# Seven products of halves in the first MLP stage of the last two units

## The chip, the cores and the metric

The kernel runs on one core of one Trainium2 chip. The metric is device time in microseconds (us), the median of several runs. TensorE does the matmuls (its weight loads have a row of their own, PEld), VectorE (DVE), ScalarE (ACT) and GpSimd (POOL) do the rest; SP issues most DMAs. L-numbers are lines of the kernel before.

## The reference

For 8 batches with 8 heads, 576 positions and 64 values per head: k and v are averaged over groups of 8 positions (72 remain), `x = softmax(q k^T / 8) v` per head, and the heads side by side give x with 576 rows of 512. Then a token MLP and a channel MLP:

```python
h  = np.maximum(xt @ w_tok1, 0.0) @ w_tok2        # over the 576 tokens, 256 hidden
u  = x + h.transpose(0, 2, 1)
h2 = np.maximum(u @ w_ch1, 0.0) @ w_ch2           # 512 -> 1536 -> 512
return u + h2
```

## The kernel before

The order of all work is written out by hand. `HEAD` lists the steps of the start. After it come nine units, 0 to 8, one for the channel MLP of 512 rows each: units 0 to 7 take 512 rows of one batch, unit 8 takes the remaining 64 rows of all eight batches (the tails). A unit is a Python generator, `unit_fast`, that stops (`yield`) after every four matmuls of 256 columns or two of 512. `PLAN[n]` maps the number of such a stop, here called a step, to other work that is put in there: `"6.av3"` is step av3 of batch 6. An engine executes its instructions in the order in which they were written down, so the position of a step is its position in the queue of every engine that it uses, DMA issues included.

**First stage of a unit.** `l1_tile` computes one of 12 tiles of `relu(u @ w_ch1)`, transposed: four matmuls of 128x512 (L517) add up in a PSUM bank, and ScalarE writes the relu to `GT` (L521). `uT` is u transposed, four chunks of 128 with 512 columns. 24 steps.

**Second stage.** It is already a product of 2x2 blocks with seven multiplications in place of eight (Winograd's form): `product` makes twelve matmuls of 256 columns (L583) for each of x, y, z, a second x, w, a second z and a third x, 21 steps. In unit 8 w is left for the end and added up in x's bank. `plus` adds the bank of a product to the residual or to an earlier sum (L626: `s` tiles and output tiles `o`). Sums of blocks of GT are made by `g_sums` on VectorE, named in the plan as `=1` to `=4` (L545, L557); those of `w_ch2` are made once, in unit 0.

**The attention steps of a later batch** fill a unit: K and V pool keys and values on GpSimd (L174 to L180), Q transposes q, s computes scores and their exponentials, av the weighted values (L379, scaled on VectorE in L384), at and u the token MLP (L393, L415, L416). From batch 3 on, uT is made over memory: M0, M2 and M4 write u out, M and MT read it back in quads of 32 rows, and T0 to T5 transpose it in blocks on VectorE (L458; T4 and T5 are the tails). l steps load the inputs of a later batch.

**gate** (`g` in the plan) is a small VectorE memset (L712) and a GpSimd copy that waits for it (L713). The next gate's memset waits for that copy, so neither engine runs far ahead of the other.

**PSUM** has eight banks: four single ones (p1a to p1d), handed out in turn by `take` and `give`, and two tiles of two banks (`ps_two`). A bank is written again when its reader is done.

Of the kernel before, what the change touches and what calls it, by code (L numbers as in the profile page):

```python
# [8 lines left out]
FP32 = mybir.dt.float32  # L9
BF16 = mybir.dt.bfloat16  # L10
U32 = mybir.dt.uint32
AF = mybir.ActivationFunctionType
# [19 lines left out]
]  # L32
# [3 lines left out]
def kernel(  # L36
# [14 lines left out]
    nc = tc.nc  # L51
    B, H, S, D = q.shape
    P = 128
    POOL = 8
    BOUNCED = range(3, B)
    SP = S // POOL
# [48 lines left out]
    qT0 = area[:, 3200:3200 + 2 * HP * EV].rearrange("m (a l n) -> m a l n", a=HP, l=2)  # L105


    values = [singles.tile([SP, H, D + 1], BF16, name=f"vp{i}") for i in range(2)]
    exps = [singles.tile([SP, H * S + BP], BF16, name=f"ex{i}") for i in range(2)]
    rests = [singles.tile([P, DM], BF16, name=f"xt{i}") for i in range(2)]  # L110
# [76 lines left out]
    def batch_steps(b):  # L187
# [136 lines left out]

        def avh(g, c):
            def go():
                cs = (c, c + 1) if c < 4 else (4,)
                ps = ps_two.tile([P, 2, 512], FP32, name="p2")
                den = outp.tile([P, 2, 4], FP32, name="den", bufs=4)
                for i, cc in enumerate(cs):  # L330
                    for h in range(4):
                        n0 = (4 * g + h) * S + cc * P
                        nc.tensor.matmul(out=ps[:, i, h * (D + 1):(h + 1) * (D + 1)], lhsT=st["ex"][:, n0:n0 + P],
                                         rhs=st["vp"][:, 4 * g + h, :], start=True, stop=True)
                view = ps[:, :, 0:4 * (D + 1)].rearrange("p a (h e) -> p a h e", e=D + 1)
                if c < 4:
                    dst = late("x")[:, c:c + 2, g * 256:(g + 1) * 256].rearrange("p c (h d) -> p c h d", d=D)
                    nc.vector.reciprocal(out=den, in_=view[:, :, :, D])
                    nc.vector.tensor_tensor(out=dst, in0=view[:, :, :, 0:D],
                                            in1=den[:, :, :, None].broadcast_to([P, 2, 4, D]), op=ALU.mult)  # L340
                else:
                    nc.vector.reciprocal(out=den[0:BP, 0], in_=view[0:BP, 0, :, D])
                    nc.vector.tensor_tensor(out=st["xt"][0:BP, g * 256:(g + 1) * 256].rearrange("p (h d) -> p h d", d=D),
                                            in0=view[0:BP, 0, :, 0:D], in1=den[0:BP, 0, :, None].broadcast_to([BP, 4, D]),
                                            op=ALU.mult)
            return go
# [22 lines left out]

        def av(c):  # L370
            def go():
                n0 = c * P if c < 4 else (8 * BP if par == 0 else 7 * BP)
                rows = slice(0, P) if c < 4 else lower
                n = rows.stop - rows.start
# [9 lines left out]
                nc.vector.tensor_tensor(out=dst.rearrange("p (a h d) -> p a h d", a=2, d=D),  # L384
                                        in0=view[:, :, :, 0:D],
                                        in1=den[rows, :, :, None].broadcast_to([n, 2, 4, D]), op=ALU.mult)
            return go
# [105 lines left out]
        for i in range(3):  # L493
            name[f"s{i}"] = scores(i)
        for c in range(5):
            name[f"av{c}"], name[f"u{c}"], name[f"t{c}"] = av(c), u(c), uT(c)
            for g in range(2):
                name[f"a{g}{c}"], name[f"m{g}{c}"] = avh(g, c), ath(g, c)
        for c in range(6):
# [14 lines left out]
    def l1_tile(n, m, uT):  # L514
        ps = take([P, 512], FP32)
        for kk in range(4):
            nc.tensor.matmul(out=ps, lhsT=w_ch1[:, kk, m * P:(m + 1) * P], rhs=uT[kk],  # L517
                             start=(kk == 0), stop=(kk == 3))
            if kk == 1:
                yield  # L520
        nc.scalar.activation(out=GT[:, m, :], in_=ps, func=AF.Relu)  # L521
        give(ps)
        yield
# [19 lines left out]

    def sub(out, a, b):
        nc.vector.tensor_tensor(out=out, in0=a, in1=b, op=ALU.subtract)  # L545

# [4 lines left out]

    def g_sums(s):
        S4 = sums_tile("S", "area")
        if s[0] == "3":
            sub(S4[:, 2], GT[:, f, lo], GT[:, f, hi])
        elif s[0] == "1":
            nc.vector.tensor_tensor(out=S4[:, 0], in0=GT[:, f, hi], in1=GT[:, sec, hi], op=ALU.add)  # L557
        elif s[0] == "2":
            sub(S4[:, 1], S4[:, 0], GT[:, f, lo])
        else:  # L560
            sub(S4[:, 3], GT[:, sec, lo], S4[:, 1])

    def weight_sum(k):
# [7 lines left out]
        else:  # L571
            sub(T[:, 3], w_ch2[:, sec, lo], T[:, 1])

    def unit_fast(n, u):
        last = n == B
        uT = [u["uT"][:, kk, :] for kk in range(4)]
        for m in range(NM):
            yield from l1_tile(n, m, uT)

# [62 lines left out]
        s1 = keep("s1")  # L642
        yield from product(x, lambda m: GT[:, m, lo], lambda m: w_ch2[:, m, lo], True,
                           plus(part(s1), part(x), residual(0, 0)), last)
        yield from product(y, lambda m: GT[:, NH + m, lo], lambda m: w_ch2[:, NH + m, lo], True,
                           plus(cols_of(oa, 0), part(y), part(s1)), end=y)
# [7 lines left out]
        if not last:  # L654
            w = bank()
            s4 = keep("s4")
            yield from product(w, lambda m: GT[:, NH + m, hi], lambda m: TW[:, 3, m], True,
                               plus(part(s4), part(w), residual(1, 0)), end=w)
# [3 lines left out]
        if last:  # L662
            yield from product(x, lambda m: SG[:, 2, m], lambda m: TW[:, 2, m], False,
                               plus(cols_of(ob, 1), part(x), part(s5), store_part(hi, [nc.scalar])), True)
            yield from product(x, lambda m: GT[:, NH + m, hi], lambda m: TW[:, 3, m], False,
                               plus(cols_of(ob, 0), part(x), residual(1, 0), store_part(lo, [nc.scalar, nc.sync])), True)
# [48 lines left out]
    def unit(n, at):  # L715
# [3 lines left out]
        for i, _ in enumerate(unit_fast(n, st)):  # L719
            for s in at.get(i, "").split():  # L720
                if s[0] == "=":
                    g_sums(s[1:])
                elif s == "g":
                    gate()
                elif s[0] == "w":
                    weight_sum(int(s[1:]))
                else:
                    b, s = s.split(".")
                    if s[0] == "l":
                        load(s[1], int(b))  # L730
                    else:
                        batches[int(b)][1][s]()

    with tc.manual_schedule(engines={PE, POOLE, DVE, ACT, SYNC}):
# [16 lines left out]
        for n in range(B + 1):  # L751
            unit(n, PLAN[n])

# [29 lines left out]
```

## Time and profile before

| | |
|---|---|
| runs | 265.91, 266.49, 267.24 us; median 266.49 |
| span of the profiled execution | 264.4 us; the runs' times lie 1.5 to 2.8 us above it |
| busy TensorE, VectorE, ScalarE, GpSimd | 256.2, 178.4, 119.6, 153.1 us |
| granted TensorE clock, mean | 0.999 |
| unit 6 begins, unit 7 begins, unit 8 begins | 196.6, 221.2, 240.7 us |
| last matmul ends, last VectorE add ends | 260.9, 261.35 us |

The time of the profiled execution is its span; what a run's own time has beyond it lies outside the instructions. A line of a group gives line, engine, operation, tiles, shape and count, then busy us and mean ns of one, then the idle time of the engine ahead of them and what ended it. A line of the timeline begins with start and length in us; instructions that follow each other are merged. The end of a matmul is modelled and reaches past the start of the next one, so starts are the better measure.

### The profile page before, as it was taken

What the parts mean: (1) busy time and instruction counts of PE and PEld (TensorE: products, weight loads), DVE (VectorE), ACT (ScalarE), POOL (GpSimd) and SP (SyncE); (2) the same over time, 40 slices, a digit from 0 to 9 for tenths busy, and PEclk for the clock granted to TensorE, in tenths of its full rate; (3) what the DMA queues carried; (4) which work ended last, traced back from release to release, by engine and by line L of the source; (5) the groups of instructions that cost most, each with busy time, mean ns of one, the idle gap of its engine ahead of it and who ended that gap; (6) DMA issues with size and microseconds to landing.
All of it is one profiled execution on the core that took longest, in us unless ns stands there. A gap on an engine that the chain in (4) does not pass through costs nothing.

```text
span 264.4 us, 5328 instructions
## 1 busy us (share of the span) xinstructions
PE 256.2 (97%) x2121; PEld 160.3 (61%) x2121; DVE 178.4 (67%) x370; ACT 119.6 (45%) x195; POOL 153.1 (58%) x177
## 2 busy tenths in 40 slices
PE   8799999989999999999999999999999999999994
PEld 3685466744677545774487447744874486486483
DVE  3557569996787655895599678844795576184183
ACT  2355763149536456425641575165435412612700
POOL 8577326899999999988959982898200010100000
PEclk9999999999999999999999999999999999999999
DMA  6999999993088928699447940830513053404104
GB/s 141 193 195 206 205 207 208 205 216 80 4 129 141 166 82 171 149 202 266 91 132 107 232 144 17 158 94 4 159 38 122 30 170 80 121 0 102 59 0 159
DMA packets 31704, 34.29 MB, mean 130 GB/s; under 512 B 3136, under 2 KB 23744, under 8 KB 31680
## 3 DMA queue, kind: packets, MB, share of 16 engines
q0 software_dynamic: 17632, 17.64, 42.3%
q1 hardware_dynamic: 13632, 15.93, 20.2%
q10 hardware_dynamic: 416, 0.39, 0.5%
q8 instruction: 16, 0.26, 0.4%
q14 instruction: 8, 0.07, 0.1%
HBM read 38.99 MB, written 12.58 MB: 195 GB/s over the span
## 4 chain that ended last, share of the span: by engine, by line
PE 73%; DVE 12%; POOL 8%; issue 3%; DMA 2%; ACT 1%; POOLq 0%; ACTq 0%
PE p1c L517 10%; PE p1b L517 8%; PE p1a L517 7%; PE p1d L517 7%; PE p1d L583 6%; PE p1c L583 5%; PE p1b L583 4%; PE p1a L583 4%; POOL t L174 3%; PE p L297 3%; DVE x L384 3%; DVE area L545 3%; PE p L379 2%; DMA kr<-in_k_dram 2%; POOL t L175 2%
## 5 line engine op out<-in xcount | busy, mean ns | idle before, releaser
L517 PEld LDWEIGHTS <-w_ch 128*128 128x128 bf16 x432 | 39.5, 98 | 44.4 <-issue 2.7
L713 POOL COPY flag<-flag 1x1 f32<-1x1 f32 x47 | 15.3, 326 | 86.0 <-DVE flag L712 86.0
L583 PEld LDWEIGHTS <-area 128*128 128x128 bf16 x432 | 41.4, 98 | 7.8 <-issue 1.2
L306 ACT ACTIVATE ex<-p 72x768 bf16<-72x768 f32 x42 | 31.6, 803 | 17.1 <-PE p L297 17.1
L583 PEld LDWEIGHTS <-GT 128*128 128x128 bf16 x324 | 30.7, 98 | 7.9 <-issue 1.6
L175 POOL TENSOR_TENSOR t<-t 72x512 f32<-72x512 f32 x23 | 31.2, 1358 | 1.8
L517 PE MATMUL p1c<-uT,w_ch 128*128 128x512 bf16 x116 | 31.4, 379 | 0.0
L521 ACT ACTIVATE GT<-p1b 128x512 bf16<-128x512 f32 x27 | 16.1, 597 | 27.5 <-PE p1b L517 20.9
L521 ACT ACTIVATE GT<-p1c 128x512 bf16<-128x512 f32 x32 | 19.1, 598 | 15.5 <-PE p1c L517 11.7
L517 PE MATMUL p1b<-uT,w_ch 128*128 128x512 bf16 x96 | 26.0, 379 | 0.0
L174 POOL TENSOR_TENSOR t<-kr 72x1024 f32<-72x1024 bf16 x12 | 25.5, 2121 | 0.4
L174 POOL TENSOR_TENSOR t<-vr 72x1024 f32<-72x1024 bf16 x11 | 23.4, 2125 | 1.0 <-DMA vr<-in_v_dram 0.5
L517 PE MATMUL p1a<-uT,w_ch 128*128 128x512 bf16 x88 | 23.9, 379 | 0.0
L517 PE MATMUL p1d<-uT,w_ch 128*128 128x512 bf16 x84 | 22.2, 379 | 0.0
L521 ACT ACTIVATE GT<-p1a 128x512 bf16<-128x512 f32 x25 | 14.9, 597 | 15.4 <-PE p1a L517 14.8
L521 ACT ACTIVATE GT<-p1d 128x512 bf16<-128x512 f32 x24 | 14.4, 599 | 12.8 <-PE p1d L517 7.3
L384 DVE TENSOR_TENSOR x<-p,den 128x512 bf16<-128x512 f32 x28 | 19.3, 691 | 1.0
L545 DVE TENSOR_TENSOR area<-GT 128x1536 bf16<-128x1536 bf16 x9 | 11.3, 1257 | 11.9 <-ACT GT L521 6.7
L557 DVE TENSOR_TENSOR area<-GT 128x1536 bf16<-128x1536 bf16 x9 | 9.5, 1054 | 11.3 <-ACT GT L521 11.3
L379 PEld LDWEIGHTS <-ex 72*128 72x128 bf16 x280 | 12.9, 98 | 6.5 <-DVE x L384 1.4
L379 PE MATMUL p<-vp,ex 72*128 72x65 bf16 x280 | 14.4, 194 | 0.3 <-POOL vp L180 0.2
L118 POOL DMA_DIRECT2D kr<-in_k_dram x17 | 10.9, 646 | 5.6 <-PE p1b L222 1.9
(185 smaller groups left out, 464.2 us busy)
## 6 DMA issues: line engine op xcount, KB each, us to landing
out_dram<-o SPq DMA_DIRECT2D x32, 256.0 KB, 4.2
qb<-in_q_dram POOLq DMA_DIRECT2D x7, 576.0 KB, 9.4
kr<-in_k_dram POOLq DMA_DIRECT2D x7, 512.0 KB, 8.4
vr<-in_v_dram POOLq DMA_DIRECT2D x7, 512.0 KB, 14.0
w_ch<-in_moe_w_ch_dram POOLq DMA_DIRECT2D x5, 512.0 KB, 14.8
mem<-u SPq DMA_DIRECT2D x10, 256.0 KB, 2.2
v<-mem SPq DMA_DIRECT2D x20, 128.0 KB, 2.9
area<-in_q_dram SPq DMA_DIRECT2D x2, 288.0 KB, 3.0
```

The lines of the kernel that those rows point to most:

```text
L118: nc.gpsimd.dma_start(out=t[j0:j1, h0:h1].rearrange("j h i d -> j h (i d)"), in_=src[b, h0:h1].rearrange("h (j i) d -> j h (i d)", i=POOL) ...
L174: eng.tensor_tensor(out=t4[:, 0:n], in0=t[:, hs, 0:4], in1=t[:, hs, 4:8], op=ALU.add)
L175: eng.tensor_tensor(out=t4[:, 0:n, 0:2], in0=t4[:, 0:n, 0:2], in1=t4[:, 0:n, 2:4], op=ALU.add)
L306: nc.scalar.activation(out=dst, in_=src, func=AF.Exp, scale=scale)
L379: nc.tensor.matmul(out=ps[:, h // 4, (h % 4) * (D + 1):(h % 4 + 1) * (D + 1)], lhsT=st["ex"][:, h * S + n0:h * S + n0 + P], rhs=st["vp"][: ...
L384: nc.vector.tensor_tensor(out=dst.rearrange("p (a h d) -> p a h d", a=2, d=D), in0=view[:, :, :, 0:D], in1=den[rows, :, :, None].broadcast ...
L517: nc.tensor.matmul(out=ps, lhsT=w_ch1[:, kk, m * P:(m + 1) * P], rhs=uT[kk], start=(kk == 0), stop=(kk == 3))
L521: nc.scalar.activation(out=GT[:, m, :], in_=ps, func=AF.Relu)
L545: nc.vector.tensor_tensor(out=out, in0=a, in1=b, op=ALU.subtract)
L557: nc.vector.tensor_tensor(out=S4[:, 0], in0=GT[:, f, hi], in1=GT[:, sec, hi], op=ALU.add)
L583: nc.tensor.matmul(out=ps[i] if split else ps[:, i], lhsT=chunk(u, i, a(m)), rhs=w(m), start=start and m == 0 and (i == 0 or split), stop= ...
L713: nc.gpsimd.tensor_copy(out=flag[:, 1:2], in_=flag[:, 0:1])
```

## The change

- In the units named in `FAST` (7 and 8, those whose uT sums y0 or Y0 stand in the plan) the first stage is also computed by seven products in place of eight. `w_ch1` is split in two halves of hidden units and two halves of inputs, uT in two halves of inputs and two of rows. `l1_fast` makes them in three groups A, B, C of four hidden tiles each. A step is four matmuls of 256 columns (`"A6"`: product 6 of group A), 21 steps in the order `ORDER`, and three empty steps behind them so that the plan's numbers stay. Per group products 1, 6, 7 and 4 add up in one bank and 2, 5 and 3 in another. ScalarE copies three interim sums to SBUF as 32-bit floats (`keep`); VectorE adds bank and copy into GT for three of the four blocks (`add`), with the relu as an in-place maximum behind it, once for groups A and B together and once for C; the fourth block is a relu on ScalarE as before.
- The copies lie in the two `ex` tiles, now 128 partitions high.
- The sums of `w_ch1` (`ch1_sum`) are four GpSimd instructions of 1536 in unit 6 (Z0 to Z3). Those of uT (`u_sum`) are y0 and y1 on VectorE, Y2 and Y3 on GpSimd for unit 7, and y0 to y3 on VectorE for unit 8.
- `GT` is laid out as two halves of rows, each contiguous, in every unit.
- The plans of units 6 to 8 are new: av0, av4, at1 earlier, at0 one step later, `=3` later, M4 behind M, MT later, T4 and T5 in unit 7's second stage. The option to scale av on ScalarE is not used by the plan.

The core of the diff:

```diff
-    {7: "7.av0", 10: "7.av4", 14: "7.at0 =3", 15: "7.at1", 17: "7.u3 7.u0", 19: "7.u1", 20: "7.u2 7.M0 7.u4", 22: "7.M2", 23: "g =1", 26: "7.M4", 27: "7.M", 28: "=2", 31: "g", 32: "g", 34: "=4", 36: "7.T1", 38: "7.T2", 39: "7.T3", 40: "7.T0", 41: "g g"},
-    {3: "7.MT", 4: "7.T4", 13: "g", 18: "g", 21: "g", 24: "=3", 25: "=1", 27: "7.T5", 28: "=2", 30: "g", 32: "=4", 42: "g", 43: "g"},
-    {22: "=3", 24: "=1", 25: "g", 26: "=2", 27: "=4", 42: "g"},
+    {1: "Z0", 4: "7.av0", 6: "7.av4", 8: "7.at1", 10: "Z1", 15: "7.at0", 16: "Z2", 17: "7.u1 7.u0 7.M0 7.u3 7.u4", 19: "7.u2", 20: "=3 Z3", 22: "7.M2", 25: "g =1", 27: "=2 7.M", 28: "g", 33: "=4", 34: "g", 35: "g 7.T3", 37: "7.T1 7.M4 7.T2", 38: "7.T0", 42: "7.y0", 43: "g 7.y1", 44: "7.Y2"},
+    {0: "g", 6: "7.MT", 12: "7.Y3", 18: "g", 21: "=1", 27: "=2", 30: "=3", 32: "=4", 34: "7.T4", 35: "7.T5", 40: "8.y0", 41: "8.y1 8.y3", 42: "8.y2"},
+    {21: "=1", 26: "=2", 29: "=4", 32: "=3"},
...
-    GT = singles.tile([P, NM, 4 * P], BF16)
+    GT = singles.tile([P, 2, NM, 2 * P], BF16)
...
+    exs = [singles.tile([P, H * S + BP], BF16, name=f"ex{i}") for i in range(2)]
+    exps = [t[0:SP] for t in exs]
+    spare = [exs[i][:, j * 1024:(j + 1) * 1024].bitcast(FP32).rearrange("p (j n) -> p j n", j=2) for i in range(2) for j in range(4)]
...
+    def ch1_sum(k, eng):
+        a11, a21 = (w_ch1[:, 0:2, i * NH * P:(i + 1) * NH * P] for i in range(2))
+        a12, a22 = (w_ch1[:, 2:4, i * NH * P:(i + 1) * NH * P] for i in range(2))
...
+            eng.tensor_tensor(out=C1[0], in0=a21, in1=a22, op=ALU.add)
+        else:
+            sub(C1[k], *((C1[0], a11), (a11, a21), (a12, C1[1]))[k - 1], eng)
...
+        sub(t[:, k], *((b12, uT[:, 0:2, lo]), (b22, t[:, 0]), (b22, b12), (b21, t[:, 1]))[k], eng)
...
+        factors = {1: (w(0, 0), b(0, lo)), 2: (w(0, 1), b(1, lo)), 3: (ws(3), b(1, hi)), 4: (w(1, 1), us(3)),
+                   5: (ws(0), us(0)), 6: (ws(1), us(1)), 7: (ws(2), us(2))}
...
+        def keep(g, k):
+            kept[g, k] = spare[len(kept) % len(spare)]
+            nc.scalar.copy(out=kept[g, k], in_=bank[g, k == 5])
+
+        def add(g, k, ps, row, half):
+            dst = GT[:, half, row * NH + 2 * g:row * NH + 2 * g + 2]
+            nc.vector.tensor_tensor(out=dst, in0=ps, in1=kept[g, k], op=ALU.add)
+            if g > 0:
+                dst = GT[:, half, row * NH + 4 * (g - 1):row * NH + 2 * g + 2]
+                nc.vector.tensor_scalar(out=dst, in0=dst, scalar1=0.0, scalar2=None, op0=ALU.max)
...
+            ps = bank[g, k in (2, 3, 5)]
+            a, c = factors[k]
+            for j in range(2):
+                for kk in range(2):
+                    nc.tensor.matmul(out=ps[:, j], lhsT=a(2 * g + j, kk), rhs=c(kk),
+                                     start=k in (1, 2, 5) and j == 0 and kk == 0, stop=kk == 1, skip_group_check=True)
+            if k == 1 or k == 5:
+                keep(g, k)
+            elif k == 6:
+                keep(g, 2)
+            elif k == 2:
+                add(g, 1, ps, 0, 0)
+            elif k == 3:
+                add(g, 2, ps, 0, 1)
+            elif k == 7:
+                add(g, 5, ps, 1, 1)
+            else:
+                nc.scalar.activation(out=GT[:, 0, NH + 2 * g:NH + 2 * g + 2], in_=ps, func=AF.Relu)
...
+    ORDER = "A1 A2 B1 B2 A6 C1 C2 A5 A7 B6 A3 B5 B7 A4 C6 B3 C5 C7 B4 C3 C4"
...
+        if n in FAST:
+            step = l1_fast(n, uT)
+            for t in ORDER.split():
+                step("ABC".index(t[0]), int(t[1]))
+                yield
+            for _ in range(3):
+                yield
+        else:
+            for m in range(NM):
+                yield from l1_tile(n, m, uT)
```

More of the change, by code (lines that the diff above doesn't have):

```diff
@@ L54 @@
     POOL = 8
-    BOUNCED = range(3, B)
+    BOUNCED = [b for b in range(B) if any(f"{b}.M" in v.split() for at in PLAN for v in at.values())]
     SP = S // POOL
@@ L105 @@
     qT0 = area[:, 3200:3200 + 2 * HP * EV].rearrange("m (a l n) -> m a l n", a=HP, l=2)
+    FAST = [int(t.split(".")[0]) for at in PLAN for v in at.values() for t in v.split() if t[1:] in (".y0", ".Y0")]
+    C1, U1 = [], {}
     values = [singles.tile([SP, H, D + 1], BF16, name=f"vp{i}") for i in range(2)]
-    exps = [singles.tile([SP, H * S + BP], BF16, name=f"ex{i}") for i in range(2)]
+    exs = [singles.tile([P, H * S + BP], BF16, name=f"ex{i}") for i in range(2)]
+    exps = [t[0:SP] for t in exs]
+    spare = [exs[i][:, j * 1024:(j + 1) * 1024].bitcast(FP32).rearrange("p (j n) -> p j n", j=2) for i in range(2) for j in range(4)]
     rests = [singles.tile([P, DM], BF16, name=f"xt{i}") for i in range(2)]
@@ L323, in score, with scaled, avh @@
             return go
-        def avh(g, c):
+        def scaled(dst, view, den, on_act):
+            if not on_act:
+                n, a = den.shape[0], den.shape[1]
+                nc.vector.tensor_tensor(out=dst, in0=view, in1=den[:, :, :, None].broadcast_to([n, a, 4, D]), op=ALU.mult)
+                return
+            for a in range(den.shape[1]):
+                for h in range(4):
+                    nc.scalar.mul(dst[:, a, h], view[:, a, h], den[:, a, h:h + 1])
+        def avh(g, c, on_act=False):
             def go():
@@ L383, in go @@
                 nc.vector.reciprocal(out=den[rows], in_=view[:, :, :, D])
-                nc.vector.tensor_tensor(out=dst.rearrange("p (a h d) -> p a h d", a=2, d=D),
-                                        in0=view[:, :, :, 0:D],
-                                        in1=den[rows, :, :, None].broadcast_to([n, 2, 4, D]), op=ALU.mult)
+                scaled(dst.rearrange("p (a h d) -> p a h d", a=2, d=D), view[:, :, :, 0:D], den[rows], on_act)
             return go
@@ L520, in l1_tile @@
                 yield
-        nc.scalar.activation(out=GT[:, m, :], in_=ps, func=AF.Relu)
+        nc.scalar.activation(out=GT[:, :, m, :], in_=ps.rearrange("p (h n) -> p h n", h=2), func=AF.Relu)
         give(ps)
@@ L542, with sub @@
     f, sec = slice(0, NH), slice(NH, NM)
-    def sub(out, a, b):
-        nc.vector.tensor_tensor(out=out, in0=a, in1=b, op=ALU.subtract)
+    def sub(out, a, b, eng=nc.vector):
+        eng.tensor_tensor(out=out, in0=a, in1=b, op=ALU.subtract)
     def sums_tile(key, name):
@@ L550, in sums_tile, with g_sums @@
         return fast[key]
-    def g_sums(s):
+    def g_sums(s, eng):
         S4 = sums_tile("S", "area")
         if s[0] == "3":
-            sub(S4[:, 2], GT[:, f, lo], GT[:, f, hi])
+            sub(S4[:, 2], GT[:, 0, f], GT[:, 1, f], eng)
         elif s[0] == "1":
-            nc.vector.tensor_tensor(out=S4[:, 0], in0=GT[:, f, hi], in1=GT[:, sec, hi], op=ALU.add)
+            eng.tensor_tensor(out=S4[:, 0], in0=GT[:, 1, f], in1=GT[:, 1, sec], op=ALU.add)
         elif s[0] == "2":
-            sub(S4[:, 1], S4[:, 0], GT[:, f, lo])
+            sub(S4[:, 1], S4[:, 0], GT[:, 0, f], eng)
         else:
-            sub(S4[:, 3], GT[:, sec, lo], S4[:, 1])
+            sub(S4[:, 3], GT[:, 0, sec], S4[:, 1], eng)
     def weight_sum(k):
@@ new lines, in u_sum, with l1_fast, w, ws @@
+    def u_sum(n, k, eng):
+        uT = batches[n][2]["uT"] if n < B else uT_tails
+        b12, b21, b22 = uT[:, 0:2, hi], uT[:, 2:4, lo], uT[:, 2:4, hi]
+        if k == 0:
+            U1[n] = raw.tile([P, 4, 2, 256], BF16, name="qb")
+        t = U1[n]
+        sub(t[:, k], *((b12, uT[:, 0:2, lo]), (b22, t[:, 0]), (b22, b12), (b21, t[:, 1]))[k], eng)
+    def l1_fast(n, uT):
+        def w(i, k):
+            return lambda m, kk: w_ch1[:, 2 * k + kk, (i * NH + m) * P:(i * NH + m + 1) * P]
+        def ws(k):
+            return lambda m, kk: C1[k][:, kk, m * P:(m + 1) * P]
+        def b(k, half):
+            return lambda kk: uT[2 * k + kk][:, half]
+        def us(k):
+            return lambda kk: U1[n][:, k, kk]
+        factors = {1: (w(0, 0), b(0, lo)), 2: (w(0, 1), b(1, lo)), 3: (ws(3), b(1, hi)), 4: (w(1, 1), us(3)),
+                   5: (ws(0), us(0)), 6: (ws(1), us(1)), 7: (ws(2), us(2))}
+        bank, kept = {}, {}
+        def keep(g, k):
[7 more added lines that the diff above has]
+                nc.vector.tensor_scalar(out=dst, in0=dst, scalar1=0.0, scalar2=None, op0=ALU.max)
+        def step(g, k):
+            if k == 1:
+                if g > 0:
+                    bank[g, 0], bank[g, 1] = (take([P, 2, 256], FP32) for _ in range(2))
+                else:
+                    bank[g, 0], bank[g, 1] = (ps_two.tile([P, 2, 512], FP32, name="p2")[:, 0].rearrange(
+                        "p (j n) -> p j n", j=2) for _ in range(2))
+            ps = bank[g, k in (2, 3, 5)]
[16 more added lines that the diff above has]
+                nc.scalar.activation(out=GT[:, 0, NH + 2 * g:NH + 2 * g + 2], in_=ps, func=AF.Relu)
+                if g == NM // 4 - 1:
+                    for i in range(4):
+                        give(bank[1 + i % 2, i // 2])
+        return step
@@ L576, in unit_fast @@
         uT = [u["uT"][:, kk, :] for kk in range(4)]
-        for m in range(NM):
-            yield from l1_tile(n, m, uT)
+        if n in FAST:
[5 more added lines that the diff above has]
+                yield
+        else:
+            for m in range(NM):
+                yield from l1_tile(n, m, uT)
         def product(ps, a, w, start, after, split=False, end=None):
@@ L642, in unit_fast @@
         s1 = keep("s1")
-        yield from product(x, lambda m: GT[:, m, lo], lambda m: w_ch2[:, m, lo], True,
+        yield from product(x, lambda m: GT[:, 0, m], lambda m: w_ch2[:, m, lo], True,
                            plus(part(s1), part(x), residual(0, 0)), last)
-        yield from product(y, lambda m: GT[:, NH + m, lo], lambda m: w_ch2[:, NH + m, lo], True,
+        yield from product(y, lambda m: GT[:, 0, NH + m], lambda m: w_ch2[:, NH + m, lo], True,
                            plus(cols_of(oa, 0), part(y), part(s1)), end=y)
@@ L656, in unit_fast @@
             s4 = keep("s4")
-            yield from product(w, lambda m: GT[:, NH + m, hi], lambda m: TW[:, 3, m], True,
+            yield from product(w, lambda m: GT[:, 1, NH + m], lambda m: TW[:, 3, m], True,
                                plus(part(s4), part(w), residual(1, 0)), end=w)
@@ L664, in unit_fast @@
                                plus(cols_of(ob, 1), part(x), part(s5), store_part(hi, [nc.scalar])), True)
-            yield from product(x, lambda m: GT[:, NH + m, hi], lambda m: TW[:, 3, m], False,
+            yield from product(x, lambda m: GT[:, 1, NH + m], lambda m: TW[:, 3, m], False,
                                plus(cols_of(ob, 0), part(x), residual(1, 0), store_part(lo, [nc.scalar, nc.sync])), True)
@@ L750 @@
             head(s)
-        for n in range(B + 1):
-            unit(n, PLAN[n])
+        for n, at in enumerate(PLAN):
+            unit(n, at)
 _INS = ['q', 'k', 'v', 'moe_w_tok1', 'moe_w_tok2', 'moe_w_ch1', 'moe_w_ch2']
```

25 lines of the change are left out of this document (16 added, 9 removed).

## The prediction

> **What bounds the kernel now.** I read the page's busy times and its 40 slices first, then the windows of the last two units, then the chain of waits, then the timeline.
>
> ```profile
> PE 256.2 (97%) x2121; PEld 160.3 (61%) x2121; DVE 178.4 (67%) x370; ACT 119.6 (45%) x195; POOL 153.1 (58%) x177
> ...
> DVE  3557569996787655895599678844795576184183
> ...
> POOL 8577326899999999988959982898200010100000
> ```
>
> TensorE is the bound everywhere. VectorE is loaded to half or more except at the end, where it has empty slices, and GpSimd has almost nothing in the last quarter. The stages that change are unit 7 (221.2 to 240.7 us) and unit 8 (from 240.7 on):
>
> ```profile
> 221.20:240.70 19.50, 19.50 (x134) 12.89 (x132) 9.94 (x25) 7.16 (x12) 1.90 (x7) 1.00 0.26 68
> 240.70:261.40 20.70, 19.90 (x134) 12.83 (x132) 9.98 (x20) 7.17 (x12) 0.52 (x3) 1.00 0.26 77
> ```
>
> Columns are the stretch, its length, then busy time of PE, PEld, DVE, ACT and POOL, granted clock, DMA. TensorE has no gap in unit 7 and one in unit 8; VectorE is half idle. The chain and the timeline show where that gap is:
>
> ```profile
> 251.35 0.61 ACT GT L521
> 251.98 0.96 DVE area L557
> 253.53 0.96 DVE area L545
> 254.57 0.81 issue
> 255.39 0.68 DVE o L626
> 256.78 1.47 PE p1d L583 x12
> ```
>
> ```profile
> 230.69 1.03 PE L517 MATMUL p1d<-uT,w_ch 128*128 128x512 bf16 x4
> 231.56 1.47 PE L583 MATMUL p1b<-w_ch,GT 128*128 128x256 bf16 x12
> ...
> 255.01 1.47 PE L583 MATMUL p<-area,area 128*128 128x256 bf16 x12
> 256.78 1.47 PE L583 MATMUL p1d<-w_ch,area 128*128 128x256 bf16 x12 [0.29 <-DVE s L626]
> ```
>
> Busy times include 0.16 us of modelled drain, so I take starts. The first stage of unit 7 starts at 221.19 and its second at 231.56: 48 matmuls of 512 columns in 10.37, 0.216 each. The second stage runs to 240.72: 84 of 256 columns in 9.16, 0.109 each. In unit 8 a product that should start at 256.32 (255.01 + 1.31) starts at 256.78, 0.46 late, behind VectorE's queue. The last VectorE add ends at 261.35, that is 40.16 after unit 7's start. Everything before 221.19 I expect at its old time, so the sum is that of these 40.16 us.
>
> **What it takes away.** Per unit 48 matmuls of 512 become 84 of 256, exactly the form of L583, each with its own weight load (98 ns, below the 109 of a matmul): 9.17 for 10.37, so 1.20 saved twice. The late product's 0.46 can also go, because the inputs of its VectorE sums are now ready earlier. TensorE alone would therefore end 2.86 earlier.
>
> **What it adds on ScalarE.** Nine copies and three relus of 128x512 for twelve relus of 0.60 (L521): the same load. Inside the order of the 21 steps (0.437 each) two steps run close behind their copy: A3 (A5 ends at 3.49, copy from 3.74 to 4.34, A3 due at 4.37) and C7. I put these at nothing.
>
> **What it adds on VectorE.** Per unit nine adds of 512 from PSUM and six in-place maxima of bf16 GT, three of 1024 and three of 512; for unit 7 two, for unit 8 four sums of uT halves. The prices:
>
> ```profile
> 195.02 0.69 DVE L626 TENSOR_TENSOR o<-p1a,s 128x512 f32<-128x512 f32 x1
> ...
> 195.63 0.76 DVE L458 STREAM_TRANSPOSE uT<-v 128x256 uint32<-128x256 uint32 x2
> ```
>
> An add of 512 takes 0.69, and the next instruction starts 0.61 after it. Where the next needs its result it starts 0.03 after its end (253.53 + 0.95, next at 254.51). By the same timeline an `=` sum has a pitch of 0.87, an `s` add or a block transpose 0.34. A uT sum is a third of an `=` sum: 0.157 fixed plus 0.80/3, 0.42, pitch 0.34. The fixed part comes from the two sizes of L626 (0.69 for 512, 0.42 for 256).
>
> The maximum has no row in this form. The nearest are:
>
> ```profile
> L690 DVE CAST qb<-area 128x576 bf16<-128x576 f32 x1 | 0.5, 459 | 1.3 <-DMA area<-in_q_dram 1.3
> L365 DVE TENSOR_SCALAR AT<-p1d 128x256 bf16<-128x256 f32 x1 | 0.4, 424 | 0.8 <-ACT AT L364 0.8
> ```
>
> The cast reads 576 x 4 bytes in 0.459 - 0.157 = 0.302, 7.6 bytes per ns; the `=` sum reads 2 x 1536 x 2 bytes in 0.80, 7.7. At that rate one source of 1024 bf16 costs 0.267 + 0.157 = 0.42 and 512 cost 0.29. Bounds: the fixed 0.16 below; above, results at the two-source rate (0.69 and 0.42), and beyond that one element per cycle like L365 (1.22 and 0.69). I take 0.42 and 0.29, since the cast is nearest: one source, in SBUF.
>
> VectorE's queue, in us after unit 7's start. The two last adds of unit 6 now stand behind two uT sums and end their turn at 1.9. Unit 7's first stage: three plain adds 1.83, six with a maximum behind them 6 x 0.72 = 4.32, maxima 3 x 0.34 + 3 x 0.29 = 1.89, waits on ScalarE and a gate 0.3: to 10.3. Its second stage: four `=` 3.48, eight `s` 2.72, four output adds 2.44, two transposes 0.68, four uT sums 1.47: to 21.1. Unit 8's first stage 8.04: to 29.1. Then `=1`, two `s`, `=2`, output add, `=4`, and the pair of `s` that holds the product of the old gap: 0.87 + 0.68 + 0.87 + 0.61 + 0.87 + 0.76 = 4.66: to 33.8. That product and the two behind it take 3 x 1.31, the last add 0.2 + 0.42: 38.3. So VectorE is never idle in these units and becomes the bound; TensorE alone would end at 37.3. The saving is 40.16 - 38.3 = 1.8, not 2.86. In TensorE's rows the missing 1.0 is waits: about 0.2 at C4 in each unit (C7's add runs from 8.23 to 8.92, C4 is due at 8.73), 0.15 at A5 of unit 8 and 0.3 at the old place.
>
> If an add costs the 0.725 of L416 (also bf16 out), 18 x 0.04 = 0.7 of the gain goes.
>
> **GpSimd.** Four weight sums of 1536 start behind the gate at 198.66, in its idle 13.03 us:
>
> ```profile
> L175 POOL TENSOR_TENSOR t<-t 72x512 f32<-72x512 f32 x23 | 31.2, 1358 | 1.8
> L174 POOL TENSOR_TENSOR t<-kr 72x1024 f32<-72x1024 bf16 x12 | 25.5, 2121 | 0.4
> ```
>
> Their slope gives 2.9, their ratio 3.2; 4 x 3.2 = 12.8, done at 211.5. TensorE reads the first at 222.9. What stands behind them is the gate at step 25, and VectorE's memset at step 28 (about 215.0) waits for that gate: nothing is lost up to 4.0 each. The uT sums Y2 and Y3 (about 1.3) have 1.7 or more before A7 and A4 need them.
>
> The sums run beside `=3` of unit 6:
>
> ```profile
> L545 DVE TENSOR_TENSOR area<-GT x9: 945/959/2560, 36.1 to 246.8; 128x1536 bf16<-128x1536 bf16 x9
> ```
>
> `=3` may take the maximum, 2.56. Starting at 211.1 it then ends at 213.7 and `=1` at 214.6, when its product is due at 214.65: nothing.
>
> **What it moves.** In unit 6 av0 and av4 come 3 and 4 steps earlier; their VectorE work ends about 0.6 before at1 reads it, with av2 and av3 ahead in the queue. Putting at0 last leaves u1 0.06 behind its relu: 0 to 0.1. The spill M2 goes 0.1 later (u2 ends at 211.1 for 211.0); the quads behind it landed by 217.4 and the first transpose runs at 218.2. M4 moves behind the quads on SP's queue and MT three steps later, behind the same stores; their transposes move from steps 4 and 27 to 34 and 35 of unit 7, some 6 us after landing. That removes VectorE's idle 6.8 us at 229.6, which had cost nothing. Gates cost 0.06 each. GT's halves are now contiguous; fixed cost and rate of `=` (0.157 and two elements per cycle) show no price for the old strides, so nothing.
>
> **The sum.** 266.49 - 1.8 = 264.7. The profiled execution's span is 264.4, its last add ends at 261.35, and 2.1 lies between span and median; that tail I leave as it is.
>
> **Rivals.** (a) VectorE does not bind: TensorE's 2.86 come whole, 263.6. For it: pitches shorter by a few per cent are enough in part. Against: 38 us of queue without a gap. Chance 0.08. (b) The maximum runs at the two-source rate: pitch +0.27 for 1024 and +0.05 for 512, 0.96 per unit, 1.9 less 0.2 of waits that it covers: 266.4, no change. For it: no row shows anything faster in results per ns. Chance 0.17. The Trainium skill, VectorE: DVE Perf Modes, section on the perf-mode tier table, gives tensor_scalar on bf16 in SBUF twice the rate of tensor_tensor (693 ns against 1224 for 2048); no run here shows it yet, and it is why (b) and (c) are not likelier. (c) Slower: the maximum runs at one element per cycle as L365 does; pitch +0.80 and +0.32, 3.4 per unit, so 6.7 less 0.2: VectorE's queue holds C4 and then unit 8's start, 271.2. It decides from a mean of about 0.9 for 1024 and 0.5 for 512. For it: the only row of that operation. Against: its source is PSUM. Chance 0.08. (d) The GpSimd sums take over 4.0: VectorE's gate at step 28 then holds unit 6's adds and transposes. At 5 it costs 0.4, at 6 it costs 1.6 and the gain is gone. For it: L545's 2.56 shows that the two engines slow each other. Against: it needs twice the row. Chance 0.05.
>
> By the Trainium skill, GPSIMD Engine Reference, key points, GpSimd contends with VectorE instructions in a two-port mode or with two SBUF inputs. By that rule the first maximum of unit 7 also runs slower beside Y3, at most 0.4 more; the sum would be 265.1. No run here shows it.
>
> **Chances.** The forecast has 0.62; it is faster by more than 0.5% (1.33 us, about what a measurement can tell) in 0.52 of it and within in 0.10, by the price of the add. With (a) faster is 0.60. Same is 0.10 + 0.17 and 0.02 of (d): 0.29. Slower is (c) and 0.03 of (d): 0.11. The range goes from (a) less 0.2 of scatter, 263.4, past (b) to 267.0, and leaves out (c) and the worse part of (d), with small tails: 0.18.
>
> **What would show it.** First stages of 9.3 to 9.7 in units 7 and 8; VectorE without idle from 217 to 257; waits of TensorE on VectorE at C4 and in the second stage of unit 8; maxima of 0.42 and 0.29; GpSimd sums of about 3.2. I am wrong if a maximum takes 0.69 or more, if VectorE idles while TensorE waits for GpSimd, or if unit 7 starts later than 221.2.

## The result, and the profile after

The changed kernel takes 264.6 us (median of 5 runs, 263.88 to 265.16) against 266.49 for the kernel before in the same comparison. The ratio is 0.9929, 95% interval 0.9907 to 0.9952: faster by 0.7%, near the forecast of 264.7. The interval reaches from 1.3 to 2.5 us gained, so these times can't tell 1.8 from 1.5 or 2.3; the profile can. The profiled execution took 265.02, its span is 263.2. From here on line numbers are those of the changed kernel: L641 is the new first stage's matmul, L680 the second stage's (L583 before), L621 the copy, L625 the add, L628 the maximum, L654 the relu, L554 and L566 the sums (L545 and L557 before), L723 the adds behind a product (L626 before), L809 the gate's memset.

The page's busy times, and two of the rows of 40 slices:

```profile
PE 254.0 (97%) x2171; PEld 167.7 (64%) x2193; DVE 195.7 (74%) x400; ACT 119.0 (45%) x195; POOL 166.1 (63%) x177
...
DVE  3557469986787665896599686863696389999994
...
POOL 8667326899999999978879992798407922100000
```

TensorE has 2.2 us less to do, VectorE 17.3 more and GpSimd 13.0 more. The empty slices of VectorE at the end (5576184183 before) are now full (6389999994): the gain was bought there. The windows of the last two units show at what price. Columns are the stretch, its length, then busy time of PE, PEld, DVE, ACT and POOL, granted clock, DMA; each line is one stage of a unit.

```profile
221.97:231.46 9.49, 9.36 (x86) 8.19 (x84) 8.94 (x21) 6.26 (x11) 2.87 (x5) 1.00 0.52 140
231.46:240.63 9.17, 9.17 (x86) 8.22 (x84) 9.10 (x20) 0.60 (x1) 0.10 (x1) 1.00 0.01 2
240.63:250.11 9.48, 9.35 (x87) 8.20 (x85) 9.27 (x20) 6.26 (x11) 0.00 (x0) 1.00 0.45 112
250.11:260.16 10.05, 9.53 (x86) 8.11 (x83) 9.16 (x18) 0.60 (x1) 0.00 (x0) 1.00 0.14 52
```

A first stage took 10.37 before and takes 9.49 and 9.48 now; unit 8's second stage went from 10.26 to 10.05. That is 0.88 + 0.89 + 0.21 = 1.98. From unit 7's start to the last VectorE add, the stretch that the prediction summed (called "the stage" below), it is 38.19 for 40.16. The medians differ by 1.9.

What is left of waiting is seen in two places. At the end of unit 7's first stage, the timeline of PE, ACT and DVE (start, length, what; steps of TensorE come every 0.44):

```profile
228.97 0.60 PE L641 MATMUL p1d<-qb,kr 128*128 128x256 bf16 x4
229.42 0.60 PE L641 MATMUL p1c<-qb,vr 128*128 128x256 bf16 x4
229.86 0.60 PE L641 MATMUL p1b<-qb,w_ch 128*128 128x256 bf16 x4
230.30 0.60 PE L641 MATMUL p1d<-uT,vr 128*128 128x256 bf16 x4
231.03 0.60 PE L641 MATMUL p1c<-qb,w_ch 128*128 128x256 bf16 x4
```
```profile
229.66 0.58 ACT L621 COPY ex<-p1d 128x512 f32<-128x512 f32 x1 [0.29 <-PE p1d L641]
```
```profile
230.28 0.69 DVE L625 TENSOR_TENSOR GT<-p1c,ex 128x512 bf16<-128x512 f32 x1
231.01 0.29 DVE L628 TENSOR_SCALAR GT<-GT 128x512 bf16<-128x512 bf16 x1
```

The five matmul lines are C5, C7, B4, C3 and C4. C5's copy ends at 230.24, C7's add needs it and runs from 230.28 to 230.97, and C4, which adds up in the bank that this add reads, starts at 231.03 instead of 230.74: 0.29 late. Unit 8 shows the same 0.28. The other place is the product that was late before. The chain that ended last (start, length, what):

```profile
253.92 0.36 DVE area L554
254.28 0.51 issue
254.78 0.76 DVE s L723 x2
255.54 0.04 issue
255.58 1.47 PE p1a L680 x12
```

It starts 0.23 late where it was 0.46 late. The rest of the lost time against 37.3, about 0.1, is in the pitches.

### The profile page after: what moved, and what is told of

It is laid out like the page before. It is cut to its first block, busy times and chain, and to the rows that moved or that the text cites. A ratio compares the mean times of both kernels' runs of the same rounds, so it can differ in the third digit from the quotient of the medians.

```text
span 263.2 us, 5488 instructions
## 1 busy us (share of the span) xinstructions
PE 254.0 (97%) x2171; PEld 167.7 (64%) x2193; DVE 195.7 (74%) x400; ACT 119.0 (45%) x195; POOL 166.1 (63%) x177
## 5 line engine op out<-in xcount | busy, mean ns | idle before, releaser
L526 PEld LDWEIGHTS <-w_ch 128*128 128x128 bf16 x336 | 30.2, 98 | 33.4 <-issue 2.7
L680 PEld LDWEIGHTS <-area 128*128 128x128 bf16 x432 | 41.4, 98 | 7.5 <-issue 1.0
L680 PEld LDWEIGHTS <-GT 128*128 128x128 bf16 x324 | 30.7, 98 | 7.5 <-issue 1.6
L526 PE MATMUL p1c<-uT,w_ch 128*128 128x512 bf16 x100 | 28.0, 379 | 0.2
L177 POOL TENSOR_TENSOR t<-kr 72x1024 f32<-72x1024 bf16 x12 | 25.5, 2121 | 0.4
L177 POOL TENSOR_TENSOR t<-vr 72x1024 f32<-72x1024 bf16 x11 | 23.4, 2123 | 2.4 <-DMA vr<-in_v_dram 1.9
L526 PE MATMUL p1b<-uT,w_ch 128*128 128x512 bf16 x75 | 21.3, 379 | 0.4 <-issue 0.2
L530 ACT ACTIVATE GT<-p1c 128x512 bf16<-128x512 f32 x26 | 15.5, 597 | 12.3 <-PE p1c L526 8.5
L526 PE MATMUL p1a<-uT,w_ch 128*128 128x512 bf16 x72 | 20.5, 379 | 0.3
L530 ACT ACTIVATE GT<-p1b 128x512 bf16<-128x512 f32 x20 | 11.9, 596 | 15.3 <-PE p1b L526 8.8
L530 ACT ACTIVATE GT<-p1d 128x512 bf16<-128x512 f32 x19 | 11.4, 599 | 14.0 <-PE p1d L526 8.5
L423 DVE TENSOR_TENSOR u<-p1d,x 128x512 bf16<-128x512 f32 x11 | 8.0, 727 | 11.9 <-PE p1d L422 11.0
L554 DVE TENSOR_TENSOR area<-GT 128x1536 bf16<-128x1536 bf16 x9 | 11.4, 1263 | 6.9 <-ACT AT L402 5.2
L680 PE MATMUL p1a<-area,area 128*128 128x256 bf16 x108 | 14.3, 273 | 0.0
```

The lines of the kernel that those rows point to most:

```text
L177: eng.tensor_tensor(out=t4[:, 0:n], in0=t[:, hs, 0:4], in1=t[:, hs, 4:8], op=ALU.add)
L423: nc.vector.tensor_tensor(out=rows_of(c), in0=blocked(ps), in1=blocked(x), op=ALU.add)
L530: nc.scalar.activation(out=GT[:, :, m, :], in_=ps.rearrange("p (h n) -> p h n", h=2), func=AF.Relu)
L554: eng.tensor_tensor(out=out, in0=a, in1=b, op=ALU.subtract)
L680: nc.tensor.matmul(out=ps[i] if split else ps[:, i], lhsT=chunk(u, i, a(m)), rhs=w(m), start=start and m == 0 and (i == 0 or split), stop= ...
```

## The experiments

Beside the profile and the times, each run gives a length of the stage, which repeats much better than the total time (last experiment). In the kernels with an added line the line numbers behind it are one or two higher.

**The plan alone** (`e1_plan_only`): no unit takes the new first stage. The moved steps of units 6 and 7 and GT's layout stay; unit 7's `=1` goes from step 21 to 24, and unit 8 has its old plan again.

```diff
-    {1: "Z0", ... 10: "Z1", ... 16: "Z2", ... 20: "=3 Z3", ... 42: "7.y0", 43: "g 7.y1", 44: "7.Y2"},
+    {... 20: "=3", ... 43: "g"},
-    {... 12: "7.Y3", ... 21: "=1", ... 40: "8.y0", 41: "8.y1 8.y3", 42: "8.y2"},
+    {... 24: "=1", ...},
-    {21: "=1", 26: "=2", 29: "=4", 32: "=3"},
+    {22: "=3", 24: "=1", 25: "g", 26: "=2", 27: "=4", 42: "g"},
```

> The changed kernel with the old first stage of twelve tiles in units 7 and 8 and without the weight and uT sums; the new order of steps and the new layout of GT stay. Theory (the gain is TensorE's shorter first stages, less what VectorE gives back): no gain, unit 7's start to the last VectorE add takes 40.1 to 40.2 us as before, the product in unit 8 is late by 0.4 to 0.5 again, VectorE idles in the first stages, time 266.5. Rival (the new order of steps or the layout brings it): 38.2 and 264.6.

Measured: 266.9, ratio 1.0014 (0.9992 to 1.0036); the stage is 40.16, equal to that before. The late product is back:

```profile
256.27 1.47 PE L680 MATMUL p1d<-w_ch,area 128*128 128x256 bf16 x12 [0.30 <-DVE s L723]
```

The moved steps of units 6 and 7 and the layout are worth nothing by themselves; the gain comes only with the new first stages. Unit 8's new order of `=` sums was always run with its new first stage, so what it does to the late product (0.21 of the 1.98) wasn't tested apart.

**One unit alone** (`e2_unit8_only`, `e3_unit7_only`): as above, with Z0 to Z3 as in the change, and the uT sums and the new first stage left to unit 8 or to unit 7. The unit without them has its `=` sums where `e1_plan_only` has them.

```diff
 e2:  -  42: "7.y0", 43: "g 7.y1", 44: "7.Y2"  /  12: "7.Y3", ... 21: "=1"
      +  43: "g"                               /  24: "=1"
 e3:  -  40: "8.y0", 41: "8.y1 8.y3", 42: "8.y2"  /  {21: "=1", 26: "=2", 29: "=4", 32: "=3"}
      +                                           /  {22: "=3", 24: "=1", 25: "g", 26: "=2", 27: "=4", 42: "g"}
```

> Seven products in unit 8 alone; unit 7 as in the kernel before. Theory: unit 7 takes 19.5; unit 8 gains 1.2 less waits on VectorE (about 0.25 at C4, 0.3 at the old place), so 39.1 to 39.2 from unit 7's start, time 265.5. Rival (VectorE does not bind, the whole of TensorE's 1.2 + 0.46 comes): 38.5, time 264.8.

> Seven products in unit 7 alone; unit 8 as in the kernel before. Theory: unit 7 takes 18.6 (1.2 less a wait of 0.2 to 0.3 at C4), unit 8 20.6 with its late product, 39.1 to 39.2 together, time 265.5; with the run of unit 8 alone the two gains add up to that of the change, about 2.0. Rival (the gain lies in unit 8 alone, where VectorE no longer stops the late product): 40.1, time 266.4.

Measured: unit 8 alone 265.71, ratio 0.9972 (0.9951 to 0.9992), stage 39.11; unit 7 alone 265.93, ratio 0.9974 (0.9951 to 0.9998), stage 39.23. The gains of 1.05 and 0.93 add up to 1.98, the change's 1.97: neither unit takes from the other.

**GT's layout** (`e8_gt_rows`): the old order of hidden tiles and halves in memory, all else as changed.

```diff
-    GT = singles.tile([P, 2, NM, 2 * P], BF16)
+    GT = singles.tile([P, NM, 2, 2 * P], BF16, name="GT").rearrange("p m h n -> p h m n")
```

> The changed kernel with GT in the old layout, the two halves of a tile side by side. Theory: an = sum costs 0.95 and a maximum 0.43 or 0.29 in either layout; the one effect is that the first product of the second stage of units 7 and 8 waits for the last VectorE write into rows that it does not read, 0.3 to 0.4 each, part of which the later waits take up: 38.3 to 38.6 from unit 7's start, time 264.8. Rival (the contiguous layout makes VectorE's sums and maxima faster): = sums over 1.0 and maxima over 0.5 here, above 39, time over 265.5.

Measured: 264.46, ratio 0.993 (0.9906 to 0.9955); stage 38.54, 0.35 longer, 0.30 of it in unit 7's second stage (9.47 for 9.17). In the total time this can't be seen. The sums and maxima take what they took (0.95, 0.43 and 0.29), so their price isn't it. The first product of the second stage takes 1.61 from its start (232.24) to the next start (233.85), instead of 1.31. This fits the expectation's wait for VectorE's last write into GT (a maximum that ends at 233.01), though the profile names no releaser. Unit 8 shows the same 0.29, of which its late product takes up 0.23. With the new first stage the contiguous halves are thus worth about 0.3, which the prediction had put at nothing; with the old one (`e1_plan_only`) they gain nothing.

**No maximum** (`e4_no_max`): three of the four blocks of GT are written without relu in units 7 and 8.

```diff
-                nc.vector.tensor_scalar(out=dst, in0=dst, scalar1=0.0, scalar2=None, op0=ALU.max)
+                pass
```

**Every maximum twice** (`e5_max_twice`): that line a second time.

> The changed kernel without the twelve VectorE maxima: three of the four blocks of GT keep their negative values. Theory (VectorE's queue and TensorE are nearly level; TensorE alone would end at 37.3): VectorE loses about 2.5 us per unit, the waits at A5 and in the second stage of unit 8 go, those at C4 stay at 0.2 since C7's add waits for ScalarE's copy: 37.7 to 37.8 from unit 7's start, time 264.1. Rival (VectorE's load does not matter): 38.2, time 264.6. Rival (VectorE is far behind TensorE): 37.3 or less is impossible for TensorE, so a gain over 0.9 refutes the whole account.

> Every maximum is made twice, which changes no value: 3 x 0.46 + 3 x 0.32 = 2.3 us more on VectorE per unit. Theory (VectorE's queue sets the end): 4.2 to 4.6 later, 42.4 to 42.8 from unit 7's start, time 268.9. Rival (VectorE runs beside TensorE with room): 38.2 to 38.7, time 264.6 to 265.1. It also stands for the prediction's case in which a maximum costs twice its price.

Measured: without, 264.76, ratio 0.9925 (0.9897 to 0.9954), stage 37.95. Twice, 268.26, ratio 1.0074 (1.0049 to 1.0098), stage 42.16. Both stages miss what was expected by about 0.2. A doubled maximum starts 0.46 (1024) or 0.32 (512) after the first, so the queue gets 6 x 0.46 + 6 x 0.32 = 4.7 longer and the stage 3.97 longer. Without the maxima the queue is about 5 shorter (2.5 per unit by the expectation) and the stage 0.24 shorter. VectorE is thus filled nearly to the edge: some 0.7 of the 4.7 found room, the rest costs in full, and the load that is there costs 0.24. Without the maxima VectorE is busy 7.65 of 9.50 and 8.00 of 9.48 in the first stages, and yet they are as long as with them:

```profile
222.62:232.12 9.50, 9.37 (x87) 8.19 (x85) 7.65 (x16) 6.26 (x11) 2.98 (x5) 1.00 0.52 140
...
241.28:250.76 9.48, 9.35 (x87) 8.19 (x84) 8.00 (x14) 6.26 (x11) 0.00 (x0) 1.00 0.45 111
```

VectorE now stands idle before C7's add, until C5's copy is done. This is unit 7's; unit 8's add, at 249.58, has the same 0.42:

```profile
230.94 0.69 DVE L625 TENSOR_TENSOR GT<-p1c,ex 128x512 bf16<-128x512 f32 x1 [0.42 <-ACT ex L621]
```

So C4's wait in both units does not need the load: the latency from C5 over the copy and the add is enough for all of it. Only the 0.24 at the late product was load. With the maxima doubled C4's wait becomes load as well, and is 1 us:

```profile
230.90 0.60 PE L642 MATMUL p1c<-qb,w_ch 128*128 128x256 bf16 x4 [0.99 <-DVE GT L625]
```

**C5 and C7 earlier** (`e9_c7_early`). If that wait is latency, starting its chain earlier should remove it.

```diff
-    ORDER = "A1 A2 B1 B2 A6 C1 C2 A5 A7 B6 A3 B5 B7 A4 C6 B3 C5 C7 B4 C3 C4"
+    ORDER = "A1 A2 B1 B2 A6 C1 C2 A5 A7 B6 A3 B5 C6 B7 C5 B3 C7 A4 B4 C3 C4"
```

> The order of the 21 steps ends on B5 C6 B7 C5 B3 C7 A4 B4 C3 C4 in place of B5 B7 A4 C6 B3 C5 C7 B4 C3 C4; nothing else is changed, the maxima stay on VectorE. C5 then comes 0.87 earlier and C7 0.44 earlier before C4. Theory 1 (the 0.29 waits at C4 are the latency of C5's copy and C7's add, since they are just as long without any maximum): both waits go, the stage is 38.19 - 0.57 = 37.6 to 37.7, the time 264.0. Theory 2 (VectorE's queue in the first stage is full, and an add that comes earlier comes behind others): C4's waits stay or grow to about 0.4, the stage is 38.2 to 38.6, the time 264.6 to 265.0. Under theory 2 the one-step-earlier C7 gains nothing because its add stands behind the adds and maxima of A and B.

Measured: 264.53, ratio 0.9923 (0.9894 to 0.9953); stage 38.59, 0.4 longer. DVE's timeline in unit 7:

```profile
227.69 0.69 DVE L625 TENSOR_TENSOR GT<-p1b,ex 128x512 bf16<-128x512 f32 x1 [0.68 <-PE p1b L641]
228.41 0.43 DVE L628 TENSOR_SCALAR GT<-GT 128x1024 bf16<-128x1024 bf16 x1
228.76 0.68 DVE L625 TENSOR_TENSOR GT<-p1a,ex 128x512 bf16<-128x512 f32 x1
229.48 0.43 DVE L628 TENSOR_SCALAR GT<-GT 128x1024 bf16<-128x1024 bf16 x1
229.82 0.68 DVE L625 TENSOR_TENSOR GT<-p1c,ex 128x512 bf16<-128x512 f32 x1
```

B7, one step later in this order, comes late enough to leave VectorE idle for 0.68; its add, a maximum, B3's add and another maximum then stand in one row without a gap, and C7's add waits its turn behind them until 229.82. That is 8.51 after the unit's start, 0.20 later than in the changed kernel (8.31), though C7 itself comes a step earlier. So theory 2: in this order the wait is the queue's. The queue and the latency lie within a few tenths of each other, and taking away one uncovers the other.

**Two uT sums from VectorE to GpSimd** (`e10_y_gpsimd`).

```diff
-  40: "8.y0", 41: "8.y1 8.y3", 42: "8.y2"},
+  39: "8.y0", 40: "8.y1", 41: "8.Y2 8.Y3"},
```

> Two of unit 8's four sums of uT halves (Y2 and Y3) go from VectorE to GpSimd, which takes 1.15 for each as in unit 7, and start two steps earlier. That takes 2 x 0.34 = 0.7 of work out of VectorE's queue in the second stage of unit 7. If VectorE's queue bounds the whole stage, the stage shortens by up to 0.7, to 37.5. If it bounds only the old place in unit 8's second stage (0.23 late) and C4's waits are latency, it shortens by 0 to 0.2: 38.0 to 38.2, time 264.4 to 264.6.

Measured: 265.23, ratio 0.9932 (0.9905 to 0.996); stage 38.18. The stage is as expected under the second theory, the time 0.6 above it. The two sums took 1.16 each on GpSimd, but a uT sum that VectorE kept ran beside the first of them (from 240.41 to 241.57) and took 0.95 instead of 0.40:

```profile
240.90 0.95 DVE L554 TENSOR_TENSOR qb<-uT_tails 128x512 bf16<-128x512 bf16 x1
```

Most of the 0.7 was lost so: VectorE's first add of unit 8 comes 2.16 after the unit's start instead of 2.28, and B7's add, which waits for a copy, comes at 6.06 in both. So this run took little load away, and says little on what 0.7 less would give.

**The maxima of groups A and B on GpSimd** (`e7_max_gpsimd`), with the order of `e9_c7_early`.

```diff
+                eng = nc.vector if g == 2 else nc.gpsimd
-                nc.vector.tensor_scalar(out=dst, in0=dst, scalar1=0.0, scalar2=None, op0=ALU.max)
+                eng.tensor_scalar(out=dst, in0=dst, scalar1=0.0, scalar2=None, op0=ALU.max)
-    {0: "g", 6: "7.MT", 12: "7.Y3", ...
+    {0: "g", 1: "7.Y3", 6: "7.MT", ...
```

> A version meant to be faster: the maxima over groups A and B run on GpSimd, which is idle there; those of C stay on VectorE; the order of the 21 steps puts C6 and C5 earlier and A4 later, so that C7's add is done when C4 is due; Y3 is issued at step 1. Theory: VectorE loses about 1.4 us per unit and the waits at C4 and A5 go: 37.5 to 37.7 from unit 7's start, 0.5 to 0.7 less than the change, time 264.0, if GpSimd takes 1.1 for 1024. If it takes 1.9, the sum =1 waits for it and 39.3 comes out, time 265.7. Rival (VectorE does not matter): 38.0 by the new order alone.

Measured: 270.17, ratio 1.0133 (1.01 to 1.0167): slower than before the change, and a miss of both expectations. The first stages run as hoped (9.20 and 9.32). For unit 7's first stage that completes the comparison: 9.49 as changed, 9.50 without maxima, 9.68 in the new order, 9.20 in the new order with only C's maxima left on VectorE. C4's wait goes only when the latency and the load are both taken away. The second stages, however, take 11.69 and 12.89, because a maximum takes GpSimd 2.77. The waits of VectorE, and the instructions of POOL and DVE behind unit 7's first stage:

```profile
DVE area L566 <- POOL GT L629: 5.3, 2, 2.7
```
```profile
227.88 5.53 POOL L629 TENSOR_SCALAR GT<-GT 128x1024 bf16<-128x1024 bf16 x2 [1.21 <-DVE GT L625]
```
```profile
233.44 0.96 DVE L566 TENSOR_TENSOR area<-GT 128x1536 bf16<-128x1536 bf16 x1 [2.65 <-POOL GT L629]
```

The sum `=1` reads the two blocks of these maxima (B7's and B3's), so VectorE stands idle until GpSimd is through at 233.41.

**Every weight sum twice** (`e6_z_twice`): rival (d) made real, each of Z0 to Z3 computed two times.

```diff
-            eng.tensor_tensor(out=C1[0], in0=a21, in1=a22, op=ALU.add)
+            for _ in range(2):
+                eng.tensor_tensor(out=C1[0], in0=a21, in1=a22, op=ALU.add)
...
+            for _ in range(2):
-            sub(C1[k], *((C1[0], a11), (a11, a21), (a12, C1[1]))[k - 1], eng)
+                sub(C1[k], *((C1[0], a11), (a11, a21), (a12, C1[1]))[k - 1], eng)
```

> Each of the four weight sums on GpSimd in unit 6 is made twice, as if one took 6.2. The prediction's price for 6 was 1.6, time 266.2. Worked out again with the trace after: the sums end at 199.4 + 24.8 = 224.2, VectorE's gate at step 28 is held from about 216 to 224.4, and the output adds, sums and transposes of unit 6 behind it, about 6 us, come only then: unit 7 starts 7 to 8 late, time 272. Rival (the sums are hidden, since TensorE reads the first only in unit 7's fifth step): 264.6.

Measured: 275.93, ratio 1.0359 (1.0338 to 1.038). The stage is 38.20; unit 7 starts at 233.43, 11.46 later than in the changed kernel. The memset of the gate at step 28 and the matmuls behind it:

```profile
226.25 0.06 DVE L811 MEMSET flag<- 1x1 f32 x1 [6.27 <-POOL flag L812]
```
```profile
228.69 2.74 PE L682 MATMUL p1c<-w_ch,area 128*128 128x256 bf16 x12 [5.86 <-DVE flag L811]
```

GpSimd works from 199.02 to 226.09, 27.1, of which 8 x 3.09 = 24.7 is the sums themselves; the rest is the mutual slowing beside `=1` and `=2` (third finding at the end). The gate's memset comes 10.1 later than in the changed kernel (216.12). The expected 272 held 7.4 for all of it. TensorE's clock adds to it: the windows of a microsecond show 0.50 granted from 227 to 233, and two products take 2.53 and 2.21 by their starts instead of 1.31 each, 2.1 more. Of these 12.2 us, 11.46 were lost; the other 0.7 would then be slack, by difference.

**The changed kernel again** (`e11_after_again`), no edit.

> The changed kernel once more, unaltered. If what precedes unit 7 scatters from run to run and the stage itself does not, the stage from unit 7's start to the last VectorE add is again 38.1 to 38.3, while unit 7 may start anywhere from 220.7 to 222.8; the ratio to the kernel before is 0.990 to 0.996. If the start at 221.97 belongs to the change, unit 7 starts at 221.9 to 222.1 again.

Measured: 264.72, ratio 0.9929 (0.9902 to 0.9956); the stage is 38.19 again, and unit 7 starts at 221.25 instead of 221.97.

## Why the prediction was right, point by point

- **Everything before unit 7 at its old time**: this step failed for the profiled execution. Unit 7 started at 221.97, 0.78 late. The loss is in batch 3's attention: the v load came 1.36 later relative to GpSimd's queue (L177 waited 1.89 for it, 0.53 before), and GpSimd's 32-bit sums then ran beside `=2` and `=4`, which took 1.36 each instead of 0.94 and 0.96. In the second profile of the same kernel they took 1.35 and 1.37 behind a wait of 1.33, and unit 7 started at 221.25; so the slower sums alone don't make the loss, and how much the load's delay makes wasn't tested. It isn't the change's doing, as that start shows, and kernels that differ from the changed one only in units 7 and 8 start it anywhere from 220.72 (`e7_max_gpsimd`) to 223.21 (`e10_y_gpsimd`). A blind sum from one profiled execution should allow for that scatter; the median hid it.
- **First stages 9.3 to 9.7**: 9.49 and 9.48. The products save 1.20 each, C4's wait takes 0.29 back (0.2 forecast).
- **Maxima of 0.42 and 0.29**: 0.43 and 0.29, so (b) and (c) fall. What slower maxima would have cost `e5_max_twice` shows: 4.7 more of them cost 3.97. Length per element: (0.428 - 0.293) / 512 = 0.26 ns, against 0.52 for the two-source sums (0.42 for 512, 0.95 for 1536). By the Trainium skill, VectorE: DVE Perf Modes, section on the perf-mode tier table, it should be half: the trace agrees.
- **Adds 0.69, copies 0.60, sums of weights 3.2, of uT 1.3**: 0.68 to 0.69, 0.58 to 0.60, 3.08 to 3.10, 1.14 to 1.15.
- **VectorE without idle, and the bound**: idle once, 0.35, and by `e5_max_twice` some 0.7 of room. The end of the sum, 38.3, is right to 0.1, but its reading isn't: the forecast put the whole distance from 37.3 to one long queue of VectorE. `e4_no_max` shows that the 0.57 at C4 stays without the load, by the latency of C5's copy and C7's add, and that 0.24 is load. The prediction had the right arithmetic for C4 (add until 8.92, C4 due at 8.73; the trace has 9.00 and 8.77) and called it a queue. That a sum over the queue alone came so close is in part luck: in unit 7 the maximum before C7's add (from 229.90, pitch 0.34) sets the queue free at 230.24, just when C5's copy ends.
- **Waits**: C4 0.29 and 0.28 for 0.2 each, A5 of unit 8 none for 0.15, the old place 0.23 for 0.3: 0.80 in all, where the forecast's items made 0.85 and its sum 1.0; the stage came out 0.1 shorter.
- **`=3` beside the weight sums may take 2.56**: it took 0.94; it started at 211.90, just after Z3 ended at 211.76.
- **The first maximum beside Y3, at most 0.4 more**: hardly tested. It took 0.43, but Y3 ended at 225.16 and the maximum began at 225.04, so they ran side by side for 0.12; what follows starts 0.42 after it because it waits for a copy that ends at 225.44. `e7_max_gpsimd` has the case: C's six maxima of 512 on VectorE run wholly beside GpSimd's and take 0.29 three times, but 0.41, 0.48 and 0.71 otherwise. The rule of the Trainium skill, GPSIMD Engine Reference, key points, is that GpSimd contends with VectorE instructions in a two-port mode or with two SBUF inputs. The sums with two SBUF inputs slow down as it says (0.95 for 0.40 in `e10_y_gpsimd`, 2.92 for 0.95 in `e6_z_twice`), and so do three of the six maxima; the mode of a maximum no trace shows.
- **Rival (a), 2.86 in full**: `e4_no_max` without any maximum reaches 37.95, not 37.3, so it was out of reach in this order of steps.
- **Rival (d)**: its limit of 4.0 was right (the gate at step 28 leaves 216.1 - 199.4 = 16.7, 4.2 each), its price wrong. It gave 0.4 at 5 and 1.6 at 6. `e6_z_twice` lost 11.5 where a sum, with its slowing, took 6.8 on average: beyond the limit every microsecond of the four sums delays the gate, and with it all of unit 6 that is left. The forecast had no harm from it, since the sums took 3.1.

## What to carry to other kernels

An engine that is nearly full costs little until the next instruction: double its suspected cost as well as removing it. Here removing gave 0.24 and doubling cost 3.97, and only the pair shows where the edge lies. Where a latency and a queue end at the same place, taking away either alone gains nothing. Where a step waits for a copy and an add behind it, moving it earlier only helps if the queue of the adding engine has a gap there. Before work goes to a second engine, look at what runs beside it there: a sum moved to GpSimd made VectorE's own sum 0.55 longer. When a total varies by 2 us from what comes before, measure the changed stage from its own start: here it repeats to 0.01 us in two executions of the same kernel.

## What had not been expected of the hardware

- GpSimd needs 2.77 us for an in-place maximum of 128x1024 bf16 with one input (2.76 to 2.80 in six), but 3.10 for a two-input sum of 128x1536: 2.7 against 2.0 ns per element. VectorE takes 0.43 for that maximum.
- After TensorE had stood still for 5.9 us in `e6_z_twice`, the granted clock was 0.50 until about 233, some 4.3 us after its next matmul had started; it had fallen some 3.4 us into the pause (the half microsecond from 226.0 shows 0.73, the pause began at 222.83).
- VectorE's two-input sums beside GpSimd's took 2.92 and 3.17 instead of 0.95, and GpSimd's up to 3.84 instead of 3.09. In `e10_y_gpsimd` a sum of 512 took 0.95 instead of 0.40 beside GpSimd's. Adds with an input from PSUM kept their 0.69 beside GpSimd's maxima; in-place maxima of 512 took 0.29 to 0.71 there.
